# Attention beside a gated MLP on one core: PV's order of pieces, one step's mask as a minimum on VectorE, and two LayerNorms begun at other places

## The chip, the cores and the metric

The kernel runs on one core of one Trainium2 chip. Its time is the device time of one execution in microseconds (us). Three runs of the kernel before gave 312.0, 312.07 and 312.23 us, median 312.07.

## The reference

The input is x (2048 rows, 640 columns, bf16). With xn = LayerNorm(x) (no scale or shift) the output is x + A(xn) + B(xn).

```python
# A: attention, 32 heads of 20, each query sees itself and the 255 keys before it
qkv = (x @ wqkv).reshape(B, S, 3, H, Dh)
scores = einsum("bhqd,bhkd->bhqk", q, k) * Dh ** -0.5
mask = (i - j >= 0) & (i - j < 256)
p = softmax(where(mask, scores, -1e9));  A = (p @ v) @ wo
# B: gated MLP, inner width 1536
B = (sigmoid(x @ w_gate) * (x @ w_up)) @ w_down
```

## The kernel before

**Tiling.** The 2048 rows are four chunks of 512 (`c` = 0 to 3). For each chunk there are projections to q and k (`g_qk`, tiles `pqk` and `st`), which go through a scratch in DRAM to change layout; to v (`g_v`, tiles `pv` and `v`); the gate and up projections (`g_gu`, tiles `pg`, `pu`; ScalarE makes `th`, a tanh, and VectorE `h = (th+1)*pu`); and the output (`g_out`: `down` over the 12 tiles of `h`, then `add_wo` over the five tiles of `oc`, both into `y`, then `add_x` on VectorE and a store). The halves that tanh and the doubled values leave are taken out by constants.

**Attention.** A chunk has eight groups of four heads, handled as four pairs of groups. Keys and queries are cut into units of 64. A pair of a chunk is worked off in steps, four in chunk 0 (table `FIRST`) and five in the others (table `LATER`): 16 + 3 x 20 = 76 steps. A step holds pieces `(j, q, n, col)`: key unit j against the n query units from q on, stored at unit `col` of the step's tile. `scores` (L471) does the matmuls into the one PSUM tile `ps` (four banks, one buffer), ScalarE takes the exponent of 8 units x 4 heads into the SBUF tile `pT` (L484), and GpSimd sets what the window cuts off to zero with four `affine_select`s (L490): two for the units on the diagonal, two for those at the window's old end, each for one half of the partitions. No maximum is subtracted. The scores of a piece are eight matmuls on separate tiles of the array (two groups, four heads); so are those of `pv`.

**PV.** When a pair's steps are done, `pv` (L494) multiplies all its pieces with v into two PSUM tiles `acc`. Its order, by the `sorted` in L497: pieces of all steps but the last first, and among them those of one or two units ahead of the longer ones; the last step's pieces at the end. In chunks 1 to 3 that gives units 2, 1, 2, 1, 5, 5, 3, 5, 3, 5, 4, 4, which are twelve pieces and 40 units; in chunk 0 nine pieces and 30 units. Then VectorE transposes each `acc` (L517); `scale_group` (reciprocals, products, another transpose to `oc`) is put into a list `fill.behind` and taken off one entry per piece of filling work.

**Order of the work.** The order on each engine is that in which the Python code issues instructions; each engine runs its own in order. `Fill` (L536) is a list of generators, the projections, the MLP and the output in a fixed order (L672 to L690), each of which yields the nominal ns of TensorE work that it issued. The main loop (L702) goes over the 76 steps: it issues PV where a pair is due (one step after the pair's last step in chunks 1 to 3, two in chunk 0), then the step's scores, exponent and masks, and then pulls filling work: at least `APART` = 1800 ns, after the last step of a pair in chunks 1 to 3 at least `LAST` = 3200 ns, and beyond that what a running `credit` allows, which spreads the filling evenly over the steps that are left.

**PSUM.** Four banks are `ps`; the other four are one pool `ps_d` for `pqk`, `pv`, `pg`, `pu`, `y` and `acc`. A new tile takes the bank whose reader was issued earliest, so TensorE waits if that reader is late.

**LayerNorm.** `g_norms(c)` (L334) yields after each block of 128 rows: four blocks of statistics (two `bn_stats`, L240, and one aggregate, L246, on VectorE), with the fourth also `rstds` for all four on GpSimd (L254, L255); two empty yields; four normalisations `xn` on VectorE (L260), for chunks 1 and 2 each with a transposing DMA on SP's queue (L271), for chunk 3 with the DMAs in `g_turns` later. `mix(a, b, first, every, rest)` puts a step of b behind each `every`-th yield of a from number `first` on. Chunk 2's norms start in "v1" and go on in "out0"; chunk 3's are in "gu1b".

**Start.** Ahead of the loop come chunk 0's LayerNorm, v and q/k (L617 to L659). TensorE runs from 6.9 us on almost without a gap.

Of the kernel before, what the change touches and what calls it, by code (L numbers as in the profile page):

```python
# [9 lines left out]
P = 128  # L10
# [10 lines left out]
HG = 4  # L21
# [11 lines left out]
SUB = mybir.AluOpType.subtract  # L33
POW = mybir.AluOpType.pow
GE = mybir.AluOpType.is_ge
BF16 = mybir.dt.bfloat16
FP32 = mybir.dt.float32
EXP = mybir.ActivationFunctionType.Exp
# [5 lines left out]
U = 64  # L44
# [22 lines left out]
LATER = (  # L67
    dict(pieces=((2, 2, 5, 2), (-3, 0, 2, 0), (7, 7, 1, 7)), diag=(2, 2), old=(1, 2), units=8),
    dict(pieces=((3, 3, 5, 1), (6, 6, 2, 6), (-4, 0, 1, 0)), diag=(1, 2), old=(0, 2), units=8),
    dict(pieces=((0, 0, 5, 3), (-2, 0, 3, 0)), diag=(3, 1), old=(2, 2), units=8),  # L70
    dict(pieces=((1, 1, 5, 0), (5, 5, 3, 5)), diag=(0, 2), old=(4, 1), units=8),
    dict(pieces=((-1, 0, 4, 0), (4, 4, 4, 4)), diag=(4, 1), old=(3, 1), units=8),
)
SPAN = 5

# [16 lines left out]
def kernel(  # L92
# [11 lines left out]
    nc = tc.nc  # L104
# [84 lines left out]
    def load_rest():  # L189
        load_gu(wg, B_w_gate, 1, 0, FS // 2)  # L190
        load_gu(wu, B_w_up, 1, 0, FS // 2)
        load_gu(wg, B_w_gate, 1, FS // 2)
        load_gu(wu, B_w_up, 1, FS // 2)
        spread("q", 0, 4, NG)
        spread("k", 0, 4, NG)
# [32 lines left out]
    for n in (6, 4):  # L228
        ps = ps_d.tile([P, CW], FP32, name="pwarm", tag="d")
        for k in range(n):  # L230
            nc.tensor.matmul(ps, lhsT=ones[:, 0:P], rhs=ones, start=(k == 0), stop=(k == n - 1))


    xnT = {}
    xns = {}
# [98 lines left out]
    def g_norms(c, turn):  # L334


        new_xnT(c)
        mvs = lnp.tile([P, SBC, nc.vector.BN_AGGR_DIM], FP32, name="mvs", bufs=1)
        for s in range(SBC):
            ln_block(c, s, mvs[:, s, :])  # L340
            if s == SBC - 1:
                rstds = rstd_blocks(mvs)
            yield 0
        yield 0
        yield 0
        for s in range(SBC):
            norm_block(c, s, mvs[:, s, :], rstds[:, s:s + 1])
            yield 0
            if turn:
                turn_block(c, s)  # L350
# [120 lines left out]
    def scores(c, o, step):  # L471
        pt = pp.tile([P, HG, PTW], BF16, name="pT")
        ps = ps_s.tile([P, HG, CW], FP32, name="ps")
        for j, q, n, col in step["pieces"]:
            kc, kb = divmod(c * CW // U + j, CW // U)
            for a in range(2):
                for i in range(HG):
                    nc.tensor.matmul(  # L478
                        ps[a * U:(a + 1) * U, i, col * U:(col + n) * U],
                        lhsT=qk["k", kc, o // GH][32 * i:32 * i + DH, o % GH + a, kb * U:(kb + 1) * U],  # L480
                        rhs=qk["q", c, o // GH][32 * i:32 * i + DH, o % GH + a, q * U:(q + n) * U],
                        start=True, stop=True)
        width = step["units"] * U
        nc.scalar.activation(out=pt[:, :, 0:width], in_=ps[:, :, 0:width], func=EXP, scale=SCALE)  # L484
        for (u, n), base, sign in ((step["diag"], 0, 1), (step["old"], -1, -1)):
            for a in range(2):
                two = pt[a * U:(a + 1) * U].rearrange("p h (a b) -> p h a b", a=2)
                k, b = divmod(u, SPAN)
                view = two[:, :, k:k + n, b * U:(b + 1) * U]
                nc.gpsimd.affine_select(out=view, in_=view, pattern=[[0, HG], [0, n], [sign, U]],  # L490
                                        compare_op=GE, fill=0.0, base=base, channel_multiplier=-sign)
        return pt

    def pv(c, o, parts):  # L494
        accs = [ps_d.tile([P, CW], FP32, name="acc", tag="d") for _ in range(2)]

        flat = [(pt, *piece) for _, _, pt, piece in sorted(  # L497
            ((k == len(parts) - 1, piece[2] > 2, pt, piece) for k, (step, pt) in enumerate(parts)
             for piece in step["pieces"]), key=lambda x: x[:2])]
        for k, (pt, j, q, n, col) in enumerate(flat):  # L500
            kb, u = divmod(c * CW // U + j, 2)
            for a, acc in enumerate(accs):
                for i in range(HG):
                    h = o // 2 * HG + i
                    nc.tensor.matmul(  # L505
                        acc[32 * i:32 * i + 32, q * U:(q + n) * U],
                        lhsT=vt[kb][a * U:(a + 1) * U, u, h * VW:h * VW + 32],
                        rhs=pt[a * U:(a + 1) * U, i, col * U:(col + n) * U],
                        start=(k == 0), stop=(k == len(flat) - 1), skip_group_check=True)
        for a, acc in enumerate(accs):  # L510
            finish_group(c, o + a, acc)
# [68 lines left out]
    def mix(a, b, first, every=1, rest=True):  # L580

        for k, cost in enumerate(a):
            yield cost
            if k >= first and (k - first) % every == 0:
                yield next(b, 0)
        if rest:
            yield from b
# [69 lines left out]
    for _ in g_qk(0):  # L657
        pass
    load_rest()  # L659

    fill = Fill()
    GU = 10 * MM
    OUT = 4 * 34 * 136
    APART = 1800
    LAST = 3200
    def later(load, *args):
        load(*args)
        yield 0

    norms1 = g_norms(1, True)  # L670
    norms2 = g_norms(2, True)
    fill.add("gu0a", mix(g_gu(0, 0, 4), norms1, 4, 1, False), 4 * GU)  # L672
    fill.add("gu0b", mix(g_gu(0, 4, 12), norms1, 0), 8 * GU)
    fill.add("x2", later(load_x, 2), 0)
# [1 line left out]
    fill.add("wd", later(load_wd), 0)  # L676
    fill.add("pads", later(clear_next), 0)
    fill.add("qk1", g_qk(1), 50 * MM)
    fill.add("v1", mix(mix(g_v(1), g_gu(1, 0, 2), 1, 2), norms2, 6, 1, False), 40 * 136 + 2 * GU)
    fill.add("out0", mix(g_out(0, g_gu(1, 2, 3)), norms2, 1, 1), OUT + GU)  # L680
    fill.add("x3", later(load_x, 3), 0)
    fill.add("qk2", g_qk(2), 50 * MM)
    fill.add("v2", mix(g_v(2), g_gu(1, 3, 7), 0, 1), 40 * 136 + 4 * GU)
    fill.add("gu1b", mix(g_gu(1, 7, 12), g_norms(3, False), 0), 5 * GU)
    fill.add("out1", mix(g_out(1, g_gu(2, 0, 1)), g_turns(3), 1, 3), OUT + GU)
    fill.add("qk3", g_qk(3), 50 * MM)
    fill.add("v3", mix(g_v(3), g_gu(2, 1, 5), 0, 1), 40 * 136 + 4 * GU)
# [14 lines left out]
    for t, (c, k, o, step) in enumerate(todo):  # L702
        if k == 0 and c > 0:
            fill.until(f"qk{c}")
        if k == 2 and c > 0:
            fill.until(f"v{c}")
        if t in due:
            fill.flush()
            pair = due[t]
            fill.hurry = pair[1] == NG - 2  # L710
            pv(*pair, parts.pop(pair))
            if pair[1] == NG - 2:
                fill.shut.discard(f"out{pair[0]}")
        parts.setdefault((c, o), []).append((step, scores(c, o, step)))
        last, label = next(x for x in cuts if t < x[0])
        credit += fill.left(label) / (last - t)
        least = LAST if c and k % len(LATER) == len(LATER) - 1 else APART
        credit -= least - fill.pull(least)
        credit = fill.pull(credit)
    fill.pull(10 ** 9)  # L720
    fill.flush()
# [64 lines left out]
```

## Time and profile before

| | |
|---|---|
| median of 3 runs | 312.07 us |
| the profiled execution | 311.93 us, of it span 310.2 us |
| busy: PE, ACT, POOL, DVE | 98%, 64%, 61%, 52% of the span |
| PE, matmuls by source, busy us | pu 59.9, pg 59.8, y (down) 56.8, pqk 46.2, scores 32.1, pv (v) 25.9, y (wo) 24.2, acc (PV) 21.8 |
| GpSimd masks | 304, 179.7 us; 64x512: 687 ns, 64x256: 459 ns in the mean |
| exponents | 76, 141.0 us; 128x2048: 1878 ns in the mean |
| granted TensorE clock | 1.000 |

A matmul's busy time holds its latency (a 128x512 takes 380 ns), while the next starts 216 ns after it: five `pg` matmuls take 1.08 us. So busy sums of PE say little. What TensorE loses is read from starts: the time from the first matmul of a block to that of the next block, against the columns in it at 216 ns per 512 (an eighth of that for scores and PV, whose eight matmuls run side by side).

### The profile page before, as it was taken

Reading aid. Unit: us, or ns where it says so; the run is one execution under the profiler, and the core shown is the slowest. Engines: PE = TensorE matmul, PEld = TensorE weight load, DVE = VectorE, ACT = ScalarE, POOL = GpSimd, SP = SyncE. Lnnn points to the kernel's source line nnn. Section 1 sums busy time; section 2 is a strip of 40 time slices with the busy share of each in tenths; the row PEclk is TensorE's granted clock in tenths of the full one; section 3 lists DMA queues with packets and bytes.
Section 4 is the critical chain, followed back from the end, with each engine's and each line's share of the span. In section 5 each row is a group of like instructions: output and inputs, shape, how many; then the busy total and the mean of one; then the engine's idle time right before and its main releaser. Section 6 shows DMA issues by size and latency. Waiting matters only on the chain.

```text
span 310.2 us, 10035 instructions
## 1 busy us (share of the span) xinstructions
PE 304.3 (98%) x4311; PEld 167.8 (54%) x4311; DVE 162.8 (52%) x327; ACT 198.7 (64%) x197; POOL 189.3 (61%) x351
## 2 busy tenths in 40 slices
PE   6999999999999999999999999999999999999996
PEld 3654444555557655554556664554546664444774
DVE  5633757639984354387836154383632517372433
ACT  6923877698854649889674547878673748769000
POOL 3000686787883868858795747658485686958100
PEclk9999999999999999999999999999999999999999
DMA  7997995975525053530024212650000210000202
GB/s 206 365 323 244 321 185 212 328 218 182 188 42 130 22 178 118 185 116 2 4 44 87 66 40 88 206 179 0 5 0 17 58 38 23 2 3 2 87 21 66
DMA packets 40461, 35.69 MB, mean 115 GB/s; under 512 B 10560, under 2 KB 39872, under 8 KB 40384
## 3 DMA queue, kind: packets, MB, share of 16 engines
q1 hardware_dynamic: 39552, 34.27, 36.6%
q10 hardware_dynamic: 864, 0.77, 0.8%
q8 instruction: 34, 0.56, 0.8%
q14 instruction: 11, 0.09, 0.1%
HBM read 23.63 MB, written 10.26 MB: 109 GB/s over the span
## 4 chain that ended last, share of the span: by engine, by line
PE 90%; POOL 4%; DVE 2%; ACT 1%; DMA 1%; issue 1%; SPq 0%; ACTq 0%
PE y L423 16%; PE pu L409 16%; PE pg L402 16%; PE pqk L287 15%; PE ps L478 8%; PE y L430 7%; PE pv L317 7%; PE acc L505 6%; POOL pT L490 4%; DVE stats L240 1%; DMA xc<-in_A_x_dram 1%; DVE v L326 1%; ACT pT L484 1%; PE pt L267 0%; ACT xn L602 0%
## 5 line engine op out<-in xcount | busy, mean ns | idle before, releaser
L490 POOL TENSOR_SCALAR_AFFINE_SELECT pT<-pT 64x512 bf16<-64x512 bf16 (+1 forms) x304 | 179.7, 591 | 97.1 <-ACT pT L484 81.8
L484 ACT ACTIVATE pT<-ps 128x2048 bf16<-128x2048 f32 (+1 forms) x76 | 141.0, 1855 | 61.6 <-PE ps L478 57.4
L413 DVE SCALAR_TENSOR_TENSOR h<-th,pu 128x512 bf16<-128x512 f32 x48 | 32.9, 685 | 58.5 <-PE pu L409 50.8
L409 PE MATMUL pu<-xnT,wu 128*128 128x512 bf16 x240 | 59.9, 380 | 0.0
L402 PE MATMUL pg<-xnT,wg 128*128 128x512 bf16 x240 | 59.8, 380 | 0.0
L423 PE MATMUL y<-wd,h 128*128 128x320 bf16 (+2 forms) x396 | 56.8, 296 | 0.1
L287 PE MATMUL pqk<-xnT,wqkv 128*128 128x512 bf16 x200 | 46.2, 381 | 0.0
L423 PEld LDWEIGHTS <-h 128*128 128x128 bf16 x396 | 36.7, 98 | 16.4 <-issue 2.4
L405 ACT ACTIVATE th<-pg 128x512 f32<-128x512 f32 x48 | 28.6, 595 | 15.1 <-PE pg L402 15.0
L402 PEld LDWEIGHTS <-wg 128*128 128x128 bf16 x240 | 22.4, 98 | 25.4 <-issue 1.4
L409 PEld LDWEIGHTS <-wu 128*128 128x128 bf16 x240 | 21.7, 98 | 25.7 <-issue 2.8
L517 DVE STREAM_TRANSPOSE t<-acc 128x512 f32<-128x512 f32 x32 | 21.1, 696 | 24.4 <-PE acc L505 24.4
L434 DVE SCALAR_TENSOR_TENSOR rows<-y,rows 128x320 bf16<-128x320 f32 x30 | 14.6, 489 | 35.5 <-PE y L430 35.5
L287 PEld LDWEIGHTS <-wqkv 128*128 128x128 bf16 x200 | 22.5, 119 | 18.7 <-issue 1.6
L478 PE MATMUL ps<-qT,kT 20*64 20x320 bf16 (+4 forms) x1440 | 32.1, 260 | 0.1
L478 PEld LDWEIGHTS <-kT 20*64 20x64 bf16 x1440 | 15.5, 103 | 26.0 <-issue 25.1
L317 PE MATMUL pv<-wqkv,xnT 128*128 128x320 bf16 x160 | 25.9, 300 | 0.0
L529 DVE TENSOR_TENSOR on<-t,rec 128x320 bf16<-128x320 f32 (+4 forms) x48 | 24.9, 519 | 1.1
L430 PE MATMUL y<-wo,oc 128*128 128x320 bf16 (+2 forms) x165 | 24.2, 296 | 0.0
L505 PE MATMUL acc<-pT,v 64*32 64x320 bf16 (+4 forms) x1440 | 21.8, 253 | 0.5 <-DVE v L326 0.4
L505 PEld LDWEIGHTS <-v 64*32 64x32 bf16 x1440 | 16.5, 92 | 7.1 <-issue 2.4
L326 DVE CAST v<-pv 64x320 bf16<-64x320 f32 x29 | 14.1, 486 | 10.8 <-PE pv L317 10.5
(45 smaller groups left out, 148.3 us busy)
## 6 DMA issues: line engine op xcount, KB each, us to landing
qT<-sq SPq DMA_DIRECT2D x16, 256.0 KB
kT<-sk SPq DMA_DIRECT2D x16, 256.0 KB
sq<-st SPq DMA_DIRECT2D x20, 128.0 KB
sk<-st SPq DMA_DIRECT2D x20, 128.0 KB
out_dram<-rows SPq DMA_DIRECT2D x15, 160.0 KB
wg<-in_B_w_gate_dram SPq DMA_DIRECT2D x4, 480.0 KB
wu<-in_B_w_up_dram SPq DMA_DIRECT2D x4, 480.0 KB
xc<-in_A_x_dram SPq DMA_DIRECT2D x3, 640.0 KB
```

The source lines that it names most:

```text
L287: nc.tensor.matmul(ps, lhsT=wt[:, m, :], rhs=xnT[c][:, d, :], start=(d == 0), stop=(d == DC - 1))
L317: nc.tensor.matmul(ps[:, 0:HALF], lhsT=xnT[c][:, d, s * P:(s + 1) * P], rhs=wqkv[:, d, 2 * D + hf * HALF:2 * D + (hf + 1) * HALF], start=( ...
L402: nc.tensor.matmul(pg, lhsT=part(wg, d, f), rhs=xnT[c][:, d, :], start=(d == 0), stop=(d == DC - 1))
L405: nc.scalar.activation(out=th, in_=pg, func=TANH, scale=0.5)
L409: nc.tensor.matmul(pu, lhsT=part(wu, d, f), rhs=xnT[c][:, d, :], start=(d == 0), stop=(d == DC - 1))
L413: nc.vector.scalar_tensor_tensor(out=h, in0=th, scalar=1.0, in1=pu, op0=ADD, op1=MULT)
L423: nc.tensor.matmul(y[:, 0:cut[1] - cut[0]], lhsT=ht[c, f][:, s * P:(s + 1) * P], rhs=wd[:, f, cut[0]:cut[1]], start=(f == 0), stop=False)
L430: nc.tensor.matmul(y[:, 0:cut[1] - cut[0]], lhsT=oc[c, m][:, s * P:(s + 1) * P], rhs=wo[:, m, cut[0]:cut[1]], start=False, stop=(m == DC - 1))
L478: nc.tensor.matmul(ps[a * U:(a + 1) * U, i, col * U:(col + n) * U], lhsT=qk["k", kc, o // GH][32 * i:32 * i + DH, o % GH + a, kb * U:(kb + ...
L484: nc.scalar.activation(out=pt[:, :, 0:width], in_=ps[:, :, 0:width], func=EXP, scale=SCALE)
L490: nc.gpsimd.affine_select(out=view, in_=view, pattern=[[0, HG], [0, n], [sign, U]], compare_op=GE, fill=0.0, base=base, channel_multiplier ...
L505: nc.tensor.matmul(acc[32 * i:32 * i + 32, q * U:(q + n) * U], lhsT=vt[kb][a * U:(a + 1) * U, u, h * VW:h * VW + 32], rhs=pt[a * U:(a + 1) ...
```

## The change

1. In `LATER` the last step loses its `diag` and `old` entries and gets `late=3`. `scores` then issues no `affine_select` for it; it returns a function that issues one VectorE minimum of units 3 and 4 of `pT` (128 x 4 x 128, bf16) with a constant tile `edge`, which holds 3e38 where the window lets a value through and 0 elsewhere. The exponents are positive, so the minimum keeps or zeroes them.
2. `make_edge` fills that tile once on GpSimd: a memset and four `affine_select`s, issued after chunk 0's loads.
3. The main loop pulls 1000 ns of filling work after such a step's scores, then issues the minimum, then pulls the rest of 1800 ns. `LAST` is gone.
4. `pv` orders its pieces anew: pieces of five units and pieces of one or two units in turn, then those of three and four, then those of the step with `late`. In chunks 1 to 3: 5, 1, 5, 1, 5, 2, 5, 2, 3, 3, 4, 4.
5. Chunk 2's norms start in "out0" instead of "v1"; chunk 3's start in "v2" (a block of statistics behind every second yield from number 9 on) and go on in "gu1b".

```diff
-    dict(pieces=((-1, 0, 4, 0), (4, 4, 4, 4)), diag=(4, 1), old=(3, 1), units=8),
+    dict(pieces=((-1, 0, 4, 0), (4, 4, 4, 4)), late=3, units=8),
...
+    edge = const.tile([P, HG, 2 * U], BF16, name="edge")
+
+    def make_edge():
+        nc.gpsimd.memset(edge, BIG)
+        for k, base, sign in ((0, -1, -1), (1, 0, 1)):
+            for a in range(2):
+                view = edge[a * U:(a + 1) * U, :, k * U:(k + 1) * U]
+                nc.gpsimd.affine_select(out=view, in_=view, pattern=[[0, HG], [sign, U]],
+                                        compare_op=GE, fill=0.0, base=base, channel_multiplier=-sign)
...
         nc.scalar.activation(out=pt[:, :, 0:width], in_=ps[:, :, 0:width], func=EXP, scale=SCALE)
+        if "late" in step:
+            u = step["late"]
+            view = pt[:, :, u * U:(u + 2) * U]
+            return pt, lambda: nc.vector.tensor_tensor(out=view, in0=view, in1=edge, op=MIN)
...
-        flat = [(pt, *piece) for _, _, pt, piece in sorted(
-            ((k == len(parts) - 1, piece[2] > 2, pt, piece) for k, (step, pt) in enumerate(parts)
-             for piece in step["pieces"]), key=lambda x: x[:2])]
+        flat = [(pt, *piece) for step, pt in parts for piece in step["pieces"] if "late" not in step]
+        long = [x for x in flat if x[3] == SPAN]
+        short = sorted((x for x in flat if x[3] < 3), key=lambda x: x[3])
+        flat = [x for pair in itertools.zip_longest(long, short) for x in pair if x] + [
+            x for x in flat if 3 <= x[3] < SPAN]
+        flat += [(pt, *piece) for step, pt in parts for piece in step["pieces"] if "late" in step]
...
     load_rest()
+    make_edge()
...
-    LAST = 3200
+    FIRST_PART = 1000
...
+    norms3 = g_norms(3, False)
...
-    fill.add("v1", mix(mix(g_v(1), g_gu(1, 0, 2), 1, 2), norms2, 6, 1, False), 40 * 136 + 2 * GU)
+    fill.add("v1", mix(g_v(1), g_gu(1, 0, 2), 1, 2), 40 * 136 + 2 * GU)
...
-    fill.add("v2", mix(g_v(2), g_gu(1, 3, 7), 0, 1), 40 * 136 + 4 * GU)
-    fill.add("gu1b", mix(g_gu(1, 7, 12), g_norms(3, False), 0), 5 * GU)
+    fill.add("v2", mix(mix(g_v(2), g_gu(1, 3, 7), 0, 1), norms3, 9, 2, False), 40 * 136 + 4 * GU)
+    fill.add("gu1b", mix(g_gu(1, 7, 12), norms3, 0), 5 * GU)
...
-        parts.setdefault((c, o), []).append((step, scores(c, o, step)))
+        pt, late = scores(c, o, step)
+        parts.setdefault((c, o), []).append((step, pt))
...
-        least = LAST if c and k % len(LATER) == len(LATER) - 1 else APART
-        credit -= least - fill.pull(least)
+        rest = APART
+        if late:
+            rest = APART - FIRST_PART + fill.pull(FIRST_PART)
+            late()
+        credit -= APART - fill.pull(rest)
```

More of the change, by code (lines that the diff above doesn't have):

```diff
@@ L35 @@
 GE = mybir.AluOpType.is_ge
+MIN = mybir.AluOpType.min
+BIG = 3.0e38
 BF16 = mybir.dt.bfloat16
@@ L491, in scores @@
                                         compare_op=GE, fill=0.0, base=base, channel_multiplier=-sign)
-        return pt
+        return pt, None
     def pv(c, o, parts):
         accs = [ps_d.tile([P, CW], FP32, name="acc", tag="d") for _ in range(2)]
-        flat = [(pt, *piece) for _, _, pt, piece in sorted(
-            ((k == len(parts) - 1, piece[2] > 2, pt, piece) for k, (step, pt) in enumerate(parts)
-             for piece in step["pieces"]), key=lambda x: x[:2])]
+        flat = [(pt, *piece) for step, pt in parts for piece in step["pieces"] if "late" not in step]
[4 more added lines that the diff above has]
+        flat += [(pt, *piece) for step, pt in parts for piece in step["pieces"] if "late" in step]
         for k, (pt, j, q, n, col) in enumerate(flat):
```

## The prediction

> **What bounds the kernel now.** I read the page's busy shares, then its chain, then the timeline around PV.
>
> ```profile
> span 310.2 us, 10035 instructions
> PE 304.3 (98%) x4311; PEld 167.8 (54%) x4311; DVE 162.8 (52%) x327; ACT 198.7 (64%) x197; POOL 189.3 (61%) x351
> PE 90%; POOL 4%; DVE 2%; ACT 1%; DMA 1%; issue 1%; SPq 0%; ACTq 0%
> ```
>
> TensorE bounds it, with a granted clock of 1.000: its streaming, its switches between kinds of matmul, and a few waits. At 1.08 us for five 512-column matmuls (216 ns each) all columns make 274 us, so some 30 us are start, switches and waits. The change adds and removes no TensorE work; it can only move those 30 us.
>
> PV and what follows it, from the timeline:
>
> ```profile
> 57.41 1.05 PE L505 MATMUL acc<-pT,v 64*32 64x128 bf16 x72
> 58.40 0.43 PE L478 MATMUL ps<-qT,kT 20*64 20x320 bf16 x24
> ...
> 113.45 1.41 PE L505 MATMUL acc<-pT,v 64*32 64x128 bf16 x96
> 114.78 0.43 PE L478 MATMUL ps<-qT,kT 20*64 20x320 bf16 x24
> ...
> 163.82 1.74 PE L505 MATMUL acc<-pT,v 64*32 64x128 bf16 x96
> 165.49 0.43 PE L478 MATMUL ps<-qT,kT 20*64 20x320 bf16 x24
> ...
> 270.55 1.65 PE L505 MATMUL acc<-pT,v 64*32 64x128 bf16 x96
> 272.12 0.43 PE L478 MATMUL ps<-qT,kT 20*64 20x320 bf16 x24
> ```
>
> Start to next start: chunk 0's PV 0.99 us for 30 units (27 ns a unit: 0.81), so 0.18 over; the later chunks' usual PV 1.34 for 40 units (1.07), so 0.27 over; the two at 163.82 and 270.55 take 1.67 and 1.57, 0.34 and 0.24 more than the usual.
>
> Where PV waits for a bank, and where the output projection waits for `h`:
>
> ```profile
> 78.82 0.83 DVE L240 BATCH_NORM_STATS2 stats<-xc 128x6 f32<-128x320 bf16 x2
> 80.90 0.99 DVE L326 CAST v<-pv 64x320 bf16<-64x320 f32 x2
> 81.43 0.24 PE L505 MATMUL acc<-pT,v 64*32 64x128 bf16 x4
> 82.04 1.02 PE L505 MATMUL acc<-pT,v 64*32 64x128 bf16 x68 [0.37 <-DVE v L326]
> ...
> 154.75 2.94 PE L423 MATMUL y<-wd,h 128*128 128x320 bf16 x18
> 154.78 1.14 DVE L260 TENSOR_SCALAR xn<-xc,mvs,rstds 128x640 bf16<-128x640 bf16 x2
> 155.84 0.67 DVE L413 SCALAR_TENSOR_TENSOR h<-th,pu 128x512 bf16<-128x512 f32 x1
> ```
>
> And a pair's last step, the one that changes:
>
> ```profile
> 144.12 0.42 PE L478 MATMUL ps<-qT,kT 20*64 20x256 bf16 x16
> 144.72 1.87 ACT L484 ACTIVATE pT<-ps 128x2048 bf16<-128x2048 f32 x1
> 146.66 2.00 POOL L490 TENSOR_SCALAR_AFFINE_SELECT pT<-pT 64x256 bf16<-64x256 bf16 x4 [0.22 <-ACT pT L484]
> 147.82 1.41 PE L505 MATMUL acc<-pT,v 64*32 64x128 bf16 x96
> ```
>
> Scores at 0, exponent from 0.60 to 2.47, GpSimd's masks to 4.54; PV starts at 3.70 and needs the masked units 0.86 us later (32 of 40 units), at 4.56. It fits by a hair, and not where GpSimd is behind.
>
> **The change part by part.** The terms are us against the profiled execution's 311.93; the median of the runs lies 0.14 above it.
>
> *PV's order: -1.1.* In the trace's single starts at 113.45 the first four pieces (2, 1, 2, 1 units, 0.16 us of columns) take 0.254; the fourth alone takes 0.102 instead of 0.027, and the weight loads behind it start late. From there a piece's eight matmuls start 8.4 ns apart (67 ns a piece), where queued ones start 3.4 ns apart: issue has run dry. Every later piece takes its columns' time. With a five (135 ns) ahead of each short piece, two pieces' issue (134 ns) fits under 162 ns. So I take off 0.09 of the 0.095 lost, in twelve PVs. Ends: 0 (issue isn't the cause) and -1.2. Chunk 0's PVs lose at most 0.02 each at their start; I count nothing.
>
> *Chunk 2's statistics out of "v1": -0.55.* At 81.43 PV waits for the bank of a `pv` tile whose copy stood behind 2.1 us of statistics. The PV there takes 1.55 against 0.98. In the new order the copy starts at about 79.8 instead of 80.90. The statistics now stand in "out0", after the 3.6 us of `scale_group` and before the `h` of the gate and up pair there. Counted on: `acc` transposed by 83.9, scaled by 87.5, four blocks of 1.02 by 91.5, `h` by 92.2. The `y` tile that takes that bank is reached at about 92.6. So that cover is 0.4; I count 0, ends 0 and +0.6. SP's queue: three of the four transposing DMAs now stand behind the first output store, the fourth behind the second, some 97 us; chunk 2's q/k starts at 108.7, so they cost nothing.
>
> *Masks off GpSimd: -0.57.* Four masks of 459 ns in each of twelve pairs, 22 us, leave GpSimd, and with them the waits at 163.82 (0.34) and 270.55 (0.24). GpSimd's other masks of a pair are needed a step later and have about 1 us of cover.
>
> *Chunk 3's norms earlier: -0.3.* At 154.75 the twelfth `down` matmul waits for the `h` behind two `xn`; with the scores delayed after it that is 0.36 + 0.13. Counting VectorE on in the new order, that `h` is still late by about 0.2. Ends: 0 and -0.5.
>
> *The minimum on the path.* The trace has none. Nearest rows: `xn`, bf16 to bf16, 128x640, 0.43 alone; the 128x512 transpose to `oc` 0.71. I take 0.45, as `xn` is nearer in kind; ends 0.43 and 0.71. It starts when the exponent is done, 2.55, so its result is there at 3.10 with 0.1 for the handshake. With the filling that is left between last scores and PV, TensorE needs it at 0.36 (scores and switch) + filling + 0.11 + 0.86. By the new order the filling is 2.13 in three pairs (needed at 3.46), 2.40 in four (3.73), 2.93 in two, 3.2 in two, and far more in the last. Cover 0.36 and more: 0. Behind it on VectorE wait `h`, q or v copies, up to 1 us; the banks they free are needed four tiles later.
>
> Here a row speaks against the change: a product of two SBUF operands on VectorE (`on`, 128x320) takes 0.49 where GpSimd is idle and 0.57 to 1.00 while a mask runs, so up to 0.5 more. GpSimd is usually done with the step before by then (146.44 against 146.59 in the stretch above), so I count +0.1 in all. The Trainium skill, "SBUF — State Buffer", section on its two physically separate sides, says that VectorE with two SBUF inputs and GpSimd exclude each other for a whole instruction on a shared port pair; by that alone every minimum that meets a mask waits for its end. The skill's "VectorE: DVE Perf Modes", errata table, would price a bf16 minimum of 512 at about 0.33 us (an estimate of 58 + 512/2 cycles at 0.96 GHz); by it the result would be there at 2.98, and the sum would stay.
>
> *A new wait: +0.7.* In "gu1b" the first `xn` of chunk 3 stands on VectorE ahead of an `h` and the pair's minimum, and needs `rstds`, which GpSimd now makes after the masks of the fourth step. With the preceding PV's end at 0: that step's exponent ends at 12.0, its masks at 14.4, `rstds` at 15.8 (0.23 + 1.04 and gaps), `xn` 16.3, `h` 17.0, minimum 17.45, ready 17.55. The pair is one of the three short ones, and TensorE needs it at 16.85. Ends: 0 and +1.2 (slow masks, minimum 0.71).
>
> *VectorE's load there: +0.1.* Statistics between v copies make one `pg` bank (behind a v copy at 9.95, wanted at 9.86) late by 0.1; ends 0 and 0.4.
>
> *make_edge: +0.15.* A memset and four masks of 0.46, run by GpSimd from 3.4 to about 5.8 us, beside the first `xn` at 4.85. Alone an `xn` takes 0.45, beside masks up to 0.79, so 0 to 0.35, on the path to the first v matmul.
>
> Sum: -1.1 - 0.55 - 0.57 - 0.3 + 0.1 + 0.7 + 0.1 + 0.15 = -1.47. 311.93 - 1.47 = 310.46 for such an execution, 310.6 for the median.
>
> **The rivals.**
>
> *B, no new wait:* GpSimd's `rstds` or VectorE are early enough. Then +0.8 falls away, and the `h` wait goes entirely: 309.6. For it: TensorE's own delays give the others time. Against: the order on VectorE has the dependence ahead of the minimum.
>
> *C, PV's order gives nothing:* the price is per short piece, wherever it stands. Then -0.4: 311.7. For it: in the trace no short piece stands behind a long one in PV. Against: chunk 0's three short pieces in a row run at 29 ns after the first.
>
> *D, the minimum is late in every pair:* VectorE, held until the exponent and then by a mask's port and an `h` ahead, gives it later than 3.10 by L. Beyond cover this costs 3(L - 0.36) + 4(L - 0.62). It eats 1.47 at L = 0.72, and the kernel is slower by 0.2% from L = 0.80; a contended minimum of 0.71 has 0.76. At L = 1.0 it costs 3.4: 314.0. For it: those 0.5 us of contention, the shorter filling. Against: GpSimd has 22 us less to do and is idle at that moment in the stretch shown.
>
> **How the numbers follow.** Forecast 0.55 (its own range 309.8 to 311.4, by the ends of the new wait, `make_edge` and PV), B 0.13, C 0.16, D 0.16. Two runs of this kernel can be told apart from about 0.2%, 0.6 us. Faster is the forecast and B, 0.68; within 0.2% is C, 0.16; slower is D, 0.16. The range takes in B's lower part and C, and D up to its beginning: 309.3 to 312.4.
>
> **What would show it.** Right: PV to the next scores takes 1.25 in chunks 1 to 3 instead of 1.34 and has no pair above 1.4 but one; the PV near 81 us runs without a break; GpSimd's busy time falls by about 20 us; VectorE shows twelve 128x512 minimums of about 0.45. A wait of about 0.7 stands inside the PV near 147 us, behind `rstds`. The first v matmul is up to 0.35 later than 6.90. Wrong: PV still at 1.34 (C); many PVs longer than 1.34, each followed back to a minimum (D); a stall of TensorE in "out0" near 92 us, which I priced at nothing.

## The result and the profile after

The changed kernel takes 310.93 us in the median of six runs (310.82 to 311.31); the kernel before, run beside it, 312.2 (312.0 to 313.29). The ratio is 0.9958, interval 0.9943 to 0.9973: 1.3 us less. The forecast was 310.6. The profiled execution takes 310.93 with a span of 309.2, against 311.93 and 310.2 before, so 1.0 less.

The page of the changed kernel: span, busy times, and the chain by engine.

```profile
span 309.2 us, 9990 instructions
PE 303.2 (98%) x4311; PEld 167.0 (54%) x4311; DVE 168.9 (55%) x339; ACT 198.5 (64%) x197; POOL 168.7 (55%) x308
PE 94%; DVE 3%; DMA 1%; ACT 0%; issue 0%; SPq 0%; DVEq 0%
```

GpSimd's busy time has fallen by 20.6 us and its 4% of the chain are gone; TensorE's share of the chain rises from 90 to 94%. VectorE has 12 instructions and 6.1 us more. Line numbers are larger than before: PV is now L526, scores L491, masks L508, the minimum L501, gate and up L415 and L422, `h` L426, `down` L436, v's copies L339.

PV and the scores after it, from the timeline of the changed kernel (start, us, engine, line, operation). These are the pairs that stood at 113.45 and 270.55:

```profile
112.83 1.33 PE L526 MATMUL acc<-pT,v 64*32 64x320 bf16 x96
114.08 0.43 PE L491 MATMUL ps<-qT,kT 20*64 20x320 bf16 x24
...
269.48 1.33 PE L526 MATMUL acc<-pT,v 64*32 64x320 bf16 x96
270.74 0.43 PE L491 MATMUL ps<-qT,kT 20*64 20x320 bf16 x24
```

Start to next start is 1.25 and 1.26, where it was 1.34 and 1.57; the one that stood at 163.82 with 1.67 takes 1.26 too. Eleven of the twelve PVs of chunks 1 to 3 read so; the twelfth is the one at 146.65 below.

The PV that waited for a bank near 81 us:

```profile
81.46 1.05 PE L526 MATMUL acc<-pT,v 64*32 64x320 bf16 x72
81.64 0.69 DVE L426 SCALAR_TENSOR_TENSOR h<-th,pu 128x512 bf16<-128x512 f32 x1 [0.84 <-PE pu L422]
82.45 0.43 PE L491 MATMUL ps<-qT,kT 20*64 20x320 bf16 x24
```

It is one unbroken piece of 0.99, and VectorE had been idle for 0.84 before its `h`: the statistics that stood there are gone.

What the change brought instead, between 137 and 149 us:

```profile
137.79 0.84 PE L330 MATMUL pv<-wqkv,xnT 128*128 128x320 bf16 x5
138.06 0.69 DVE L426 SCALAR_TENSOR_TENSOR h<-th,pu 128x512 bf16<-128x512 f32 x1
138.80 1.24 PE L422 MATMUL pu<-xnT,wu 128*128 128x512 bf16 x5 [0.17 <-DVE h L426]
139.71 0.94 DVE L339 CAST v<-pv 64x320 bf16<-64x320 f32 x2
139.97 0.42 PE L491 MATMUL ps<-qT,kT 20*64 20x320 bf16 x16
140.70 1.24 PE L415 MATMUL pg<-xnT,wg 128*128 128x512 bf16 x5 [0.30 <-DVE v L339]
...
145.26 1.04 POOL L268 TENSOR_TENSOR rstds<-rstds,neghalf 128x4 f32<-128x4 f32 x1
146.34 0.45 DVE L273 TENSOR_SCALAR xn<-xc,mvs,rstds 128x640 bf16<-128x640 bf16 x1 [2.34 <-POOL rstds L268]
146.65 1.54 PE L526 MATMUL acc<-pT,v 64*32 64x320 bf16 x96
146.71 0.68 DVE L426 SCALAR_TENSOR_TENSOR h<-th,pu 128x512 bf16<-128x512 f32 x1
147.30 0.42 DVE L501 TENSOR_TENSOR pT<-pT,edge 128x512 bf16<-128x512 bf16 x1
148.12 0.43 PE L491 MATMUL ps<-qT,kT 20*64 20x320 bf16 x24
```

Chunk 3's statistics, now in "v2", stand ahead of an `h` and of a v copy on VectorE, and both give their PSUM banks back late. From the `pv` block at 137.79 to `pu` is 1.01 instead of the 0.68 that five 320-column matmuls take: 0.32. From the scores at 139.97 to `pg` is 0.73, 0.37 too many. Then VectorE stands idle for 2.34 us at `xn`, for which GpSimd's `rstds` is late; behind it wait `h` and the pair's minimum, and the PV at 146.65 takes 1.47 to the next start, 0.21 more than its siblings.

The wait of the output projection for `h` near 155 us:

```profile
154.49 0.72 DVE L273 TENSOR_SCALAR xn<-xc,mvs,rstds 128x640 bf16<-128x640 bf16 x1
154.79 2.78 PE L436 MATMUL y<-wd,h 128*128 128x320 bf16 x18
155.13 1.26 DVE L426 SCALAR_TENSOR_TENSOR h<-th,pu 128x512 bf16<-128x512 f32 x2
157.51 0.42 PE L491 MATMUL ps<-qT,kT 20*64 20x320 bf16 x16
```

One `xn` and not two stands ahead of the `h` pieces. By starts, the 18 matmuls take 2.71 where an undisturbed block of 18 takes 2.55: 0.17 of the wait is left. Before, the block took 2.87 and the scores behind the `pg` block at 158.80 waited another 0.13, which they no longer do: 0.28 less in all.

The last matmul ends at 305.95 instead of 307.41, so 1.46 earlier. But the span ends 3.25 us behind it, before 2.81: 0.44 is given back there, where no work of the change stands. The last experiment comes back to this.

### The profile page after: what moved, and what is told of

It reads as the page before. It is cut to its first block, busy times and chain, and to the rows that moved or that the text cites. A ratio compares the mean times of both kernels' runs of the same rounds, so it can differ in the third digit from the quotient of the medians.

```text
span 309.2 us, 9990 instructions
## 1 busy us (share of the span) xinstructions
PE 303.2 (98%) x4311; PEld 167.0 (54%) x4311; DVE 168.9 (55%) x339; ACT 198.5 (64%) x197; POOL 168.7 (55%) x308
## 4 chain that ended last, share of the span: by engine, by line
PE 94%; DVE 3%; DMA 1%; ACT 0%; issue 0%; SPq 0%; DVEq 0%
PE y L436 18%; PE pu L422 17%; PE pg L415 17%; PE pqk L300 15%; PE ps L491 8%; PE y L443 7%; PE pv L330 7%; PE acc L526 6%; DVE on L550 1%; DMA xc<-in_A_x_dram 1%; DVE stats L253 1%; DVE v L339 1%; DVE h L426 0%; PE pt L280 0%; ACT xn L623 0%
## 5 line engine op out<-in xcount | busy, mean ns | idle before, releaser
L508 POOL TENSOR_SCALAR_AFFINE_SELECT pT<-pT 64x512 bf16<-64x512 bf16 (+1 forms) x256 | 157.1, 614 | 113.9 <-ACT pT L497 101.7
L415 PE MATMUL pg<-xnT,wg 128*128 128x512 bf16 x240 | 59.8, 380 | 0.3 <-DVE v L339 0.3
L426 DVE SCALAR_TENSOR_TENSOR h<-th,pu 128x512 bf16<-128x512 f32 x48 | 32.7, 684 | 50.0 <-PE pu L422 44.4
L422 PE MATMUL pu<-xnT,wu 128*128 128x512 bf16 x240 | 59.8, 380 | 0.2 <-DVE h L426 0.2
L436 PE MATMUL y<-wd,h 128*128 128x320 bf16 (+2 forms) x396 | 56.8, 295 | 0.0
L436 PEld LDWEIGHTS <-h 128*128 128x128 bf16 x396 | 36.7, 98 | 15.9 <-issue 2.0
L415 PEld LDWEIGHTS <-wg 128*128 128x128 bf16 x240 | 22.3, 98 | 26.1 <-issue 2.3
L422 PEld LDWEIGHTS <-wu 128*128 128x128 bf16 x240 | 22.0, 98 | 25.8 <-issue 2.4
L491 PE MATMUL ps<-qT,kT 20*64 20x320 bf16 (+4 forms) x1440 | 32.1, 260 | 0.0
L491 PEld LDWEIGHTS <-kT 20*64 20x64 bf16 x1440 | 15.4, 103 | 25.5 <-issue 24.7
L550 DVE TENSOR_TENSOR on<-t,rec 128x320 bf16<-128x320 f32 (+4 forms) x48 | 26.2, 547 | 1.1
L339 DVE CAST v<-pv 64x320 bf16<-64x320 f32 x29 | 14.1, 485 | 12.6 <-PE pv L330 12.3
L526 PE MATMUL acc<-pT,v 64*32 64x320 bf16 (+4 forms) x1440 | 20.3, 253 | 0.0
L330 PEld LDWEIGHTS <-xnT 128*128 128x128 bf16 x160 | 14.5, 98 | 8.8 <-issue 1.0
```

The lines of the kernel that those rows point to most:

```text
L330: nc.tensor.matmul(ps[:, 0:HALF], lhsT=xnT[c][:, d, s * P:(s + 1) * P], rhs=wqkv[:, d, 2 * D + hf * HALF:2 * D + (hf + 1) * HALF], start=( ...
L415: nc.tensor.matmul(pg, lhsT=part(wg, d, f), rhs=xnT[c][:, d, :], start=(d == 0), stop=(d == DC - 1))
L422: nc.tensor.matmul(pu, lhsT=part(wu, d, f), rhs=xnT[c][:, d, :], start=(d == 0), stop=(d == DC - 1))
L426: nc.vector.scalar_tensor_tensor(out=h, in0=th, scalar=1.0, in1=pu, op0=ADD, op1=MULT)
L436: nc.tensor.matmul(y[:, 0:cut[1] - cut[0]], lhsT=ht[c, f][:, s * P:(s + 1) * P], rhs=wd[:, f, cut[0]:cut[1]], start=(f == 0), stop=False)
L491: nc.tensor.matmul(ps[a * U:(a + 1) * U, i, col * U:(col + n) * U], lhsT=qk["k", kc, o // GH][32 * i:32 * i + DH, o % GH + a, kb * U:(kb + ...
```

## The experiments

Theory: the gain is made of PV's order and of three waits removed; the shape of what is left is set by VectorE's and GpSimd's load near 140 us, and the minimum is covered. Rivals: the order gives nothing by itself; the minimum or the shorter filling costs; the norms' new places give nothing. In the traces, "over its siblings" means a PV's start to the next start beyond 1.26; a view that ends inside a group shows fewer matmuls than there are (67 of 68 and 16 of 24 below).

The ratios tell the smaller differences apart only in part. The changed kernel's interval, 0.9943 to 0.9973, overlaps those of the runs with the masks back, with either LayerNorm back and with the statistics in "qk2". In time alone, differences of 0.4 to 0.8 us from the changed kernel are therefore not settled; the waits behind them are read from one trace of each kernel.

### PV's order alone

On the kernel before (the last step is `LATER[-1]` there):

```diff
-        flat = [(pt, *piece) for _, _, pt, piece in sorted(
...
+        flat = [(pt, *piece) for step, pt in parts for piece in step["pieces"] if step is not LATER[-1]]
+        long = [x for x in flat if x[3] == SPAN]
+        short = sorted((x for x in flat if x[3] < 3), key=lambda x: x[3])
+        flat = [x for pair in itertools.zip_longest(long, short) for x in pair if x] + [
+            x for x in flat if 3 <= x[3] < SPAN]
+        flat += [(pt, *piece) for step, pt in parts for piece in step["pieces"] if step is LATER[-1]]
```

> The kernel before with the new order of PV's pieces alone: masks, filling and norms as before. Theory (issue runs dry behind four short pieces in a row): each of the twelve PVs of chunks 1 to 3 loses 0.08 us of its 1.34, start to next start 1.26; 1.0 us in all, about 311.1 against 312.1. The waits at 81.4, 155, 164 and 270 us stay. Rival (a price for each short piece wherever it stands): PV stays at 1.34 and the time at 312.1.

Measured: 311.29 against 312.08, ratio 0.9977 (0.9965 to 0.999). The timeline of TensorE in this run:

```profile
113.48 1.33 PE L508 MATMUL acc<-pT,v 64*32 64x320 bf16 x96
114.74 0.43 PE L478 MATMUL ps<-qT,kT 20*64 20x320 bf16 x24
...
160.18 0.42 PE L478 MATMUL ps<-qT,kT 20*64 20x256 bf16 x16 [0.34 <-ACT pT L484]
...
269.87 1.61 PE L508 MATMUL acc<-pT,v 64*32 64x320 bf16 x96
271.41 0.43 PE L478 MATMUL ps<-qT,kT 20*64 20x320 bf16 x24
```

PV has its 1.26, so rival C of the prediction falls. Of the 0.97 that this is worth in twelve PVs 0.65 is left at the last matmul (306.76). A TensorE that is earlier meets the masks on GpSimd at their old times: the scores at 160.18 now wait 0.41 for an exponent (0.13 before), and the PV at 269.87 still takes 1.54, 0.28 over its siblings. The wait of 0.34 at 163.82 is gone in exchange, and 0.07 (PV at 200.9) and 0.14 (scores near 280) have come: a wait for GpSimd moves when TensorE's pace changes.

### All fives ahead, then the short pieces

```diff
-        flat = [x for pair in itertools.zip_longest(long, short) for x in pair if x] + [
+        flat = long + short + [
```

> The changed kernel with PV's order 5, 5, 5, 5, 1, 1, 2, 2, 3, 3, 4, 4 in chunks 1 to 3 (chunk 0: 5, 5, 5, 5, 1, 1, 2, 3, 3). Theory (four short pieces in a row use up what is queued for TensorE, wherever in PV they stand): 0.05 to 0.08 us in each of twelve PVs come back, 1.31 to 1.34 start to next start, 311.5 to 311.9 against 310.9. Rival 1 (it was the start of PV on short pieces that cost): 1.26 as in the changed kernel and 310.9. Rival 2 (each short piece costs by itself, and alternation hid nothing): the same, 310.9, but then order_alone would have shown nothing either, so only the place of the loss inside PV is open.

Measured: 312.21 against 312.07, ratio 1.0004 (0.9995 to 1.0012): the order's gain is gone, and 0.3 of the 1.3 us more is lost in chunk 0. Timeline of TensorE:

```profile
113.20 1.42 PE L526 MATMUL acc<-pT,v 64*32 64x320 bf16 x96
114.54 0.43 PE L491 MATMUL ps<-qT,kT 20*64 20x320 bf16 x24
```

Eleven of the twelve PVs are back at 1.35, though four pieces of five units (0.54 us of columns) now stand ahead of the short ones; the twelfth, at 147.2, waits for its minimum and stays at 1.48. Chunk 0's four PVs, which lost at most 0.02 before with their three short pieces first and a five behind them, now lose 0.08 each, with the three behind the fives and pieces of three units after them. So it is not the start of PV alone that costs. Four short pieces in a row cost 0.08 to 0.09 at PV's start and behind the fives alike; what stands behind a row counts too, as chunk 0 shows, and alternating with fives hides it.

The single starts show where the time goes. At 113.20 the first two short pieces behind the fives take 28 and 29 ns, their columns' time; the third takes 129 instead of 54. From it on a piece's eight matmuls start 8 to 9 ns apart, some 67 ns a piece, as they did behind the four short pieces before the change; that is more than the columns of a piece of one or two units take (27 and 54). The four short pieces together take 0.253 here and took 0.254 there, for 0.162 of columns. So issue looks late here too, after two short pieces.

### The masks back on GpSimd

The last step's `diag` and `old` entries, GpSimd's masks and `LAST` = 3200 as before; PV's order and the norms as changed.

```diff
-    dict(pieces=((-1, 0, 4, 0), (4, 4, 4, 4)), late=3, units=8),
+    dict(pieces=((-1, 0, 4, 0), (4, 4, 4, 4)), diag=(4, 1), old=(3, 1), units=8),
...
-    make_edge()
...
-        rest = APART
-        if late:
-            rest = APART - FIRST_PART + fill.pull(FIRST_PART)
-            late()
-        credit -= APART - fill.pull(rest)
+        least = LAST if c and k % len(LATER) == len(LATER) - 1 else APART
+        credit -= least - fill.pull(least)
```

> The changed kernel with the last step's masks on GpSimd again (four each), 3200 ns of filling behind its scores, and no edge tile; PV's order and the norms stay changed. Theory: GpSimd is late again for two or three PVs: 0.5 to 0.7 more, about 311.5 against 310.9; PVs without a wait take 1.26. Rival (what the minimum saves on GpSimd is lost by holding VectorE): no difference from 310.9.

Measured: 311.35 against 312.08, ratio 0.9971 (0.996 to 0.9982), 0.4 slower than the changed kernel. Timeline of TensorE near 147 us:

```profile
146.93 1.11 PE L526 MATMUL acc<-pT,v 64*32 64x320 bf16 x80
148.20 0.29 PE L526 MATMUL acc<-pT,v 64*32 64x256 bf16 x4 [0.16 <-POOL pT L508]
148.72 0.40 PE L526 MATMUL acc<-pT,v 64*32 64x256 bf16 x12 [0.24 <-POOL pT L508]
149.05 0.43 PE L491 MATMUL ps<-qT,kT 20*64 20x320 bf16 x24
```

With `rstds` ahead of it on GpSimd the pair's masks come late, and the last pieces wait twice: 2.12 from start to next start, 0.86 over the siblings. Further waits stand at 158.4 (0.41), 200.7 (0.07), 269.7 (0.29) and 279 (0.14). At the last matmul (306.55) the minimum with its shorter filling is worth 0.6; 0.25 of that goes at the end of the program, which is 3.0 behind the last matmul here.

This trace shows something else. Chunk 3's statistics still stand in "v2" here, and yet the two waits of the changed kernel at 138 and 140 us (0.32 and 0.37) are absent: from `pv` to `pu` it is 0.69, from the scores to the next block 0.36. They need both the statistics in "v2" and the minimum with its shorter filling; this run changes masks and filling together and doesn't say which of those two.

### Chunk 2's statistics back in "v1"

```diff
-    fill.add("v1", mix(g_v(1), g_gu(1, 0, 2), 1, 2), 40 * 136 + 2 * GU)
+    fill.add("v1", mix(mix(g_v(1), g_gu(1, 0, 2), 1, 2), norms2, 6, 1, False), 40 * 136 + 2 * GU)
```

> The changed kernel with chunk 2's statistics in v1 again. Theory: PV near 81 us waits for the bank of a v copy that stands behind statistics, 0.55 to 0.6 more, about 311.5 against 310.9, and out0 is as before. Rival (the lighter VectorE in out0 gives it back): 310.9.

Measured: 311.34 against 312.07, ratio 0.9985 (0.997 to 1.0), 0.4 slower than the changed kernel. Timeline of TensorE:

```profile
81.62 0.32 PE L526 MATMUL acc<-pT,v 64*32 64x320 bf16 x4
82.23 1.01 PE L526 MATMUL acc<-pT,v 64*32 64x320 bf16 x67 [0.29 <-DVE v L339]
```

The stall of 0.57 is back, with the same releaser, and the last matmul ends 0.56 later (306.51). In this execution the wait for `h` near 155 us (0.17) is absent, but TensorE was already 0.16 late at the first PV; the end of the program is 3.16 behind the last matmul, 0.1 less than in the changed kernel, which is part of why less than 0.57 shows in the time.

### Chunk 3's norms back in "gu1b"

```diff
-    fill.add("v2", mix(mix(g_v(2), g_gu(1, 3, 7), 0, 1), norms3, 9, 2, False), 40 * 136 + 4 * GU)
+    fill.add("v2", mix(g_v(2), g_gu(1, 3, 7), 0, 1), 40 * 136 + 4 * GU)
```

> The changed kernel with chunk 3's LayerNorm back in gu1b. Theory (the statistics between the v copies, and rstds ahead of the minimum, make TensorE wait at 138, 140 and 147 us, 0.32 + 0.37 + 0.21): these 0.9 go, and the wait of the down matmuls for h near 155 us grows back from 0.21 to about 0.5: 0.6 less, about 310.3 against 310.9. Rival (these waits come from the shorter filling ahead of PV and from VectorE held by the minimum): they stay, and with the h wait it is 311.2.

Measured: 311.54 against 312.08, ratio 0.997 (0.9953 to 0.9986), so 0.6 slower than the changed kernel, and not faster as I expected. The waits at 138, 140 and 147 are gone, as the theory had it. The timeline shows what replaced them:

```profile
153.80 1.67 PE L436 MATMUL y<-wd,h 128*128 128x320 bf16 x11
154.72 1.64 DVE L273 TENSOR_SCALAR xn<-xc,mvs,rstds 128x640 bf16<-128x640 bf16 x2
157.01 1.12 PE L436 MATMUL y<-wd,h 128*128 128x320 bf16 x7 [1.54 <-DVE h L426]
```

The twelfth `down` matmul waits 1.7 us for an `h` behind two `xn`, which take 0.9 and 0.8 beside GpSimd's masks. I had counted 0.5, about what the kernel before lost (0.32 + 0.13 by starts); but TensorE comes here about a microsecond earlier (153.80 for 154.75), the two `xn` do not (154.72 for 154.78), and they take 1.64 instead of 1.14. Three of the twelve runs took 310.25 to 310.30, so the wait isn't in every execution.

### Chunk 3's statistics earlier still

All four blocks and `rstds` in "qk2", ahead of v's copies:

```diff
-    fill.add("qk2", g_qk(2), 50 * MM)
-    fill.add("v2", mix(mix(g_v(2), g_gu(1, 3, 7), 0, 1), norms3, 9, 2, False), 40 * 136 + 4 * GU)
+    fill.add("qk2", mix(g_qk(2), norms3, 5, 1, False), 50 * MM)
+    fill.add("v2", mix(g_v(2), g_gu(1, 3, 7), 0, 1), 40 * 136 + 4 * GU)
```

> The changed kernel with chunk 3's four blocks of statistics and rstds in qk2, behind its k blocks, which ScalarE copies; the normalisations stay in gu1b. Theory: VectorE has room there, rstds is made 30 us before it is needed, so the 0.9 us of waits between 138 and 147 us go and the h wait near 155 us with most of them: 1.0 to 1.1 less, about 309.8 against 310.9. Rival: the statistics move the lateness to the q/k and first v copies and TensorE waits between 115 and 128 us: 0.3 less or nothing.

Measured: 310.12 against 312.08, ratio 0.9938 (0.9921 to 0.9954), 0.8 less than the changed kernel; a second series of the same kernel gave 309.98, ratio 0.9936 (0.9914 to 0.9958). The timeline at the place where the changed kernel had its late `xn`:

```profile
146.01 0.43 DVE L501 TENSOR_TENSOR pT<-pT,edge 128x512 bf16<-128x512 bf16 x1
146.13 1.33 PE L526 MATMUL acc<-pT,v 64*32 64x320 bf16 x96
147.38 0.43 PE L491 MATMUL ps<-qT,kT 20*64 20x320 bf16 x24
```

The minimum follows the exponent, the PV takes 1.25, and between 130 and 160 us TensorE has no wait left. The last matmul ends at 305.05, 0.9 earlier than in the changed kernel, which is the 0.32 + 0.37 + 0.21 of its three new waits. (The 0.17 near 155 us is gone as well, and a wait of 0.20 in `down` at 82.8 has come.) In "v2", with the shorter filling, the same statistics cost 0.9, in "qk2" nothing that the trace shows.

### The minimum four times

On the kernel just shown; the minimum is repeated with the same values.

```diff
-            return pt, lambda: nc.vector.tensor_tensor(out=view, in0=view, in1=edge, op=MIN)
+            return pt, lambda: [nc.vector.tensor_tensor(out=view, in0=view, in1=edge, op=MIN)
+                                for _ in range(4)]
```

> norms3_qk2 with the minimum issued four times over the same units (the result is the same), so each is ready 1.28 us later. Theory: the trace of norms3_qk2 shows the late pieces 0.58 to 0.70 us behind the minimum's end in the three pairs with the shortest filling, 0.74 to 0.97 in four, 1.4 and more in the others, of which 0.05 is the handshake; so 0.63 to 0.75 are lost in three pairs and 0.36 to 0.59 in four, 3.8 in all, about 313.9 against 310.1. By the cover of my prediction (0.36 and 0.62) it would be 5.4, 315.5. Rival (VectorE held back makes banks late as well): more than 6, over 316.

Measured: 315.39 against 312.07, ratio 1.0113 (1.0094 to 1.0132): 5.3 more than with one. Timeline of TensorE, and of VectorE, near 202 us:

```profile
202.05 1.11 PE L527 MATMUL acc<-pT,v 64*32 64x320 bf16 x80
203.47 0.41 PE L527 MATMUL acc<-pT,v 64*32 64x256 bf16 x16 [0.32 <-DVE pT L501]
203.81 0.40 PE L491 MATMUL ps<-qT,kT 20*64 20x320 bf16 x16
```

```profile
201.62 1.80 DVE L501 TENSOR_TENSOR pT<-pT,edge 128x512 bf16<-128x512 bf16 x4 [0.23 <-ACT pT L497]
```

Three more minimums make the result 1.38 later (0.46 from start to start), and the last 16 matmuls wait for it: 1.76 to the next start, 0.50 over the siblings. Seven PVs wait, by 0.80, 0.83, 0.76, 0.51, 0.44, 0.49 and 0.73, together 4.56; another 0.9 stands at 289.6, where `down` waits for an `h` behind the four. My theory had 3.8 in the PVs: seven times the 0.10 by which the result is later than the 1.28 I took makes most of the difference. The 0.9 in `down` I had not counted, and it is chance that the total, 5.3, comes near the 5.4 of the prediction's cover. With "qk2" one minimum is covered in every pair, 1.38 more is not covered in seven of twelve.

### The long filling kept with the minimum

`LAST` = 3200 after a pair's last step, the minimum still after the first 1000, on the kernel with the statistics in "qk2":

```diff
-        rest = APART
+        rest = least = LAST if late else APART
         if late:
-            rest = APART - FIRST_PART + fill.pull(FIRST_PART)
+            rest = least - FIRST_PART + fill.pull(FIRST_PART)
             late()
-        credit -= APART - fill.pull(rest)
+        credit -= least - fill.pull(rest)
```

> norms3_qk2 with at least 3200 ns of filling behind the scores of a pair's last step, as before the change, the minimum at its place. Theory: the minimum has 0.58 us of cover or more with 1800, so the longer filling adds only cover: 310.1, within 0.2. Rival (the even spread of the filling is itself worth something): 0.4 or more above, 310.5 or later.

Measured: 310.49 against 312.07, ratio 0.995 (0.9933 to 0.9967). Its interval overlaps that of the short filling (0.9921 to 0.9954), so neither a loss nor a gain by the long one is settled. The median lies by the rival's 310.5, but the trace speaks of single waits: the last matmul ends 0.24 later (305.29). The timeline shows one large new wait (and one of 0.13 at the scores near 159 us):

```profile
199.57 1.68 PE L526 MATMUL acc<-pT,v 64*32 64x320 bf16 x96
201.18 0.43 PE L491 MATMUL ps<-qT,kT 20*64 20x320 bf16 x24
```

1.61 to the next start, 0.35 over the siblings. The trace names no releaser; the v copies that give PV its bank end at 199.8 on VectorE and 200.5 on ScalarE, and I read the wait as theirs.

### The end of the program

In the traces so far, the time from the last matmul to the end of the span is 2.8 to 3.0 us in the three kernels with 351 GpSimd instructions (before, the order alone, the masks back) and 3.2 to 3.3 in the seven with 308. Part of the spread lies ahead of GpSimd's first closing drain. From that drain (2.30 to 2.50 behind the last matmul) to the end of the span it is 0.50 to 0.51 in the three and 0.81 to 0.95 in the seven. In each of the seven an instruction packet of 8 KB on queue q14 starts 0.28 to 0.49 us behind the end of the span; the three have none there. To test whether the length of GpSimd's program is the cause, 43 memsets of a 128x1 tile were put behind `make_edge`, on the kernel with the statistics in "qk2", and that kernel was run beside it again:

```diff
+        pad = const.tile([P, 1], FP32, name="pad")
+        for _ in range(43):
+            nc.gpsimd.memset(pad, 0.0)
```

> norms3_qk2 with 43 memsets of one column on GpSimd behind make_edge, where GpSimd is idle; with them it runs about as many instructions as before the change (351). It tests the 0.45 us that every kernel with the minimum loses behind the last matmul: there GpSimd's closing drain comes 0.3 later, beside an instruction packet of 8 KB. Theory (the length of GpSimd's program decides where its last instructions must be fetched): the span ends 2.8 to 3.0 behind the last matmul instead of 3.2, 0.2 to 0.4 less, 309.8 against 310.1. Rival (it belongs to the minimum or to edge itself): 3.2 stays, 310.1.

> norms3_qk2 once more, beside qk2_pad on one chip: 310.1, and 0.9935 to 0.9940 of the kernel before.

Measured: with the memsets 309.7 (309.32 to 309.77), ratio 0.9914 (0.9895 to 0.9932); without 309.98 (309.87 to 311.61), ratio 0.9936 (0.9914 to 0.9958). The intervals overlap, though no run with the memsets is as long as the shortest without. The trace is clearer: the end is 2.81 behind the last matmul with them, 3.26 without (0.50 and 0.94 behind GpSimd's first closing drain); the medians differ by less, 0.28. The DMA queues from 306 to 309 us, a window that reaches beyond the ends of both spans (307.8 and 308.6), first with the memsets, then without (queue, kind, packets, MB, share of 16 engines):

```profile
q10 hardware_dynamic: 144, 0.03, 5.0%
q1 hardware_dynamic: 74, 0.02, 3.0%
```

```profile
q1 hardware_dynamic: 144, 0.05, 6.6%
q10 hardware_dynamic: 150, 0.04, 5.4%
q14 instruction: 1, 0.01, 1.0%
```

GpSimd's last drain comes at 2.54 behind the last matmul with the memsets and takes 39 ns; without, at 2.84, and takes 183. So the 0.44 at the end of the changed kernel hangs on how many instructions GpSimd has, and more of them, early and empty, take it away. That queue q14 follows GpSimd's program fits one more row: only the run with the memsets has a q14 packet at 13.2 us; in all others the first behind the start comes at 45 us or later. But the late packet starts 3.55 behind the last matmul, when that drain has been over for 0.5. What the drain waits for is not shown, and how the place of the boundary depends on the count stays open.

## Why the prediction was right, and where its terms were off

| term | forecast | in the traces |
|---|---|---|
| PV's order | -1.1 | -0.97 |
| chunk 2's statistics out of "v1" | -0.55 | -0.57 |
| masks off GpSimd | -0.57 | -0.57 |
| chunk 3's norms earlier (wait for `h`) | -0.3 | -0.28 |
| minimum, contention | +0.1 | 0 |
| wait behind `rstds` | +0.7 | +0.21 |
| VectorE's load in "v2" | +0.1 | +0.69 |
| `make_edge` | +0.15 | +0.03 |
| end of the program | not named | +0.44 |
| sum | -1.47 | -1.02 |

**The direction and the gains.** Faster was right, and by the mechanisms named: the four gains came to -2.39 against -2.52 forecast. PV takes 1.26 and not 1.25 because 0.081 and not 0.09 is won in each. That an emptied issue is the reason stands less firm than the size: the run with all fives ahead loses the 0.09 again in places where, by "two pieces' issue fits under 162 ns", a filled queue should have helped. The 8 to 9 ns between starts there speak for late issue all the same; how much is queued ahead, no run measures. And the masks' -0.57 is the sum of two waits at their places in the kernel before. With the order alone one of the two went by itself and others came, so this is not what late masks cost at any pace of TensorE.

**The new wait was put in the wrong place.** "A new wait: +0.7" had the path right (`rstds`, `xn`, `h`, minimum), and "VectorE's load there: +0.1" had the bank right (a `pg` behind a v copy). The second was the large one: a block of statistics takes 1.1 us on VectorE, and of two banks behind such blocks I counted one, by 0.1. They cost 0.32 and 0.37. Those 0.69 delayed TensorE, and I take it that the late `rstds` cost only 0.21 six microseconds later for that reason; no run separates the two. Together 0.90 against 0.80 forecast: two terms on one path, whose shares were wrong, and that their sum came out near is in part luck. The run with the statistics in "qk2" takes both away, and gains the 0.9. The statistics are not the whole cause: with the masks back on GpSimd and the longer filling, the two bank waits are absent with the same statistics in "v2".

**The minimum.** Priced at 0.45, ready 3.10 after the scores' start and needed at 3.46: its cover was to be 0.36. The tile's answer from the changed kernel (min, median and max ns):

```profile
L501 DVE TENSOR_TENSOR pT<-pT,edge x12: 418/425/427, 94.7 to 285.8; 128x512 bf16<-128x512 bf16 x12
```

It takes 0.425 in the median. Apart from the one behind `rstds` it starts 0.03 behind the exponent's end and is done 2.83 to 2.93 after the scores' start, because the exponent begins at 0.50 to 0.60 and not always at 0.60; TensorE comes to the pieces that need it at 3.51 to 3.53 in the undisturbed short pairs. With the 0.05 that passes from the minimum's end to the start of a waiting matmul (at 147 us) the cover is 0.6, not 0.36, and 0.9 or more in the longer pairs. For the kernel to be slower, rival D needed every minimum 0.80 later than 3.10 (its L); four minimums, 1.38 later, show what it looks like. The Trainium skill, "VectorE: DVE Perf Modes", section on the TRN2 errata, gave an estimate of 0.33; measured is 0.425, and the measurement decides. The same section says that this row of its table is too low and puts the fixed part at about 150 cycles instead of 58; the estimate is then 0.42.

Contention with GpSimd's masks was small but not absent. With the longer filling three minimums met a mask; the clearest:

```profile
161.22 0.46 POOL L508 TENSOR_SCALAR_AFFINE_SELECT pT<-pT 64x256 bf16<-64x256 bf16 x1
161.25 0.69 DVE L501 TENSOR_TENSOR pT<-pT,edge 128x512 bf16<-128x512 bf16 x1
```

It takes 0.26 more than 0.425, with 0.43 of the mask still to run when it starts. The others there (128.38 and 267.63) take 0.15 and 0.12 more, with 0.32 and 0.29 to run; with the statistics in "qk2" the one at 128.62 takes 0.15 more, with 0.32 to run, and the same in the second series and with the 43 memsets. In the changed kernel one minimum, at 94.73, starts with 0.10 of a mask to run and takes no longer. So by the trace's times, what is added is the rest of the mask less 0.17, and nothing where less than that is left. The skill's "SBUF — State Buffer", section "SBUF: two separate sides", has VectorE with two SBUF inputs and GpSimd exclude each other for a whole instruction. These rows agree in that the minimum waits for the mask, but the wait is shorter than the rest of the mask from the minimum's recorded start. All of it stayed within the cover.

**`make_edge`.** The first `xn` beside GpSimd's four masks takes 0.56 instead of 0.45, as bounded. The first v matmul is not later for it (6.81, before 6.90), and the first q/k matmul comes at 13.46 instead of 13.43: 0.03.

**What no term had.** The end of the program. I counted GpSimd's 43 instructions fewer as time that leaves a queue, and looked for their effect where the masks had stood; the span's last 3 us were in no row that I read. Without these 0.44 the profiled execution would have lain at 310.5, on the forecast's 310.46. That it would have been so near is luck too: 0.59 too little for VectorE's load is made up by 0.49 too much for `rstds` and 0.22 too much for contention and `make_edge`.

**The rivals.** B (no new wait, 309.6) did not occur, but the run with the statistics in "qk2" is its case: 310.12, and 309.7 with the end mended. C is refuted by the order alone. Best of all kernels run is that with the statistics in "qk2" and the 43 memsets, 0.9% under the kernel before.

## What to carry to other kernels

When TensorE is at 98%, read it by starts: what a block takes from its first start to the next block's, against its columns; every gain and every loss here is such a difference. Work moved on VectorE can cost where it stands ahead of a PSUM bank's reader: count the bank of every tile behind it, not the first alone, and count it at the pace that TensorE will have after the change. And a gain on the bounding engine is handed back in part wherever the others keep their old times, so its size must be read at the end of the program and not at the place where it is made.

## What was not expected of the hardware

The end of the program depends on the number of GpSimd's instructions: with 308 it is 3.16 to 3.33 us behind the last matmul, with 351 2.81 to 3.00, and 43 empty memsets in the first microseconds take one kernel from 3.26 to 2.81. Four PV pieces of one or two units in a row cost 0.08 to 0.09 us even behind 0.54 us of queued columns. A minimum of 128x512 that meets a mask is longer by the rest of that mask less 0.17 us, in all four meetings at different places. And an `xn` of 128x640 that takes 0.45 alone takes up to 0.91 beside GpSimd's masks (two of them stand ahead of the `h` in the wait of 1.7).
